# Interleaving two stages of a fused attention and MoE kernel batch by batch, with units of 256 and 320 tokens

## The chip, the cores and the metric

One core of one Trainium2 chip runs the whole program. The metric is device time in microseconds of one execution; a kernel's time is the median of its runs. The engines are TensorE (PE; its weight loads are PEld), VectorE (DVE), ScalarE (ACT), GpSimd (POOL) and SyncE (SP, which issues the DMAs).

## The reference

Three layers follow one another for 4 batches of 576 tokens: causal attention with 8 heads of 64, a gated MoE of width 512 to 1024, and a second MoE that mixes tokens.

```python
scores = np.where(causal, -1000000000.0, scale * q @ k.T + np.minimum(bias, 0.0))
attn = softmax(scores) @ v
x_prev = np.concatenate([zeros, x[:, :-1, :]], axis=1)
xk = mu_k * x + (1.0 - mu_k) * x_prev
xr = mu_r * x + (1.0 - mu_r) * x_prev
k = np.maximum(xk @ w_k, 0.0)
x = 1.0 / (1.0 + np.exp(-(xr @ w_r))) * (k * k @ w_v)
h = np.maximum(x @ w_in, 0.0)
u, v = h[..., :512], h[..., 512:]
v_n = (v - mu) / np.sqrt(var + 1e-06)
v_s = np.einsum('ts,bsd->btd', w_spatial, v_n) + b_spatial[None, :, None]
out = (u * v_s) @ w_out
```

The third layer needs all 576 tokens of one batch (the `einsum` runs over tokens), but nothing of another batch.

## The kernel before

*Precision.* Most products are made of fp16 pairs: an operand is scaled by a power of two and split into a high and a low part (`two_parts`, L652 and L653), and three matmuls give high x high, high x low and low x high. The scales come from the largest absolute value (`power_of_two`, L307 to L320): a reduce on VectorE, a broadcast matmul against the identity, four short VectorE steps.

*Attention* is a list of `steps`: loads and splits of a head, items and products with the values. An item (`do_item`) makes the scores of one head (TensorE), finds the row minimum (VectorE, L454), takes the exponential (ScalarE, L459), divides (L471, L474), writes a high part (L496) and a low part (VectorE, L500) and transposes both by DMA (L502). G0 items hold the first 256 tokens, G1 items tokens 256 to 511, T items the last 64 of two heads. `pv` multiplies with the values (L552, L534) and writes x.

*First MoE.* It runs over nine units of 256 tokens, in the order A0, A1, B0, B1, A2, A3, B2, T, B3: A is the first 256 tokens of a batch, B the next 256, T the last 64 of all four. The first two use fp32 matmuls, the others fp16 pairs. `prep_mix` makes the mixes, then come 20 groups: 8 of `moe_A` (L754), 4 of `moe_B` (the gate, always fp32, L796) and 8 of `moe_C` (L822). A loop over these 180 groups sets the order of the work: after each, `target` says how many attention steps have to be done by then, and jobs that bring in weights are fed in between. Results go to memory (`x2_d`).

*Value sizes.* `value_sizes` loads the values of all batches and reduces them (L341) once, early.

*Second MoE.* When every unit is done, the pools of attention and of the first MoE are closed, and the four batches follow: `moe_Dv` (the half that is normalised, 128 tokens at a time, 512 columns, L1316; its `evac` is the chain L1324 to L1335 on ScalarE and VectorE), `moe_Du` (L1350), `moe_E` (over tokens, L1374), `split_g`, `moe_F` (L1402) and a store. The last 64 tokens of two batches share one tile of `moe_Dv`, so there are 18 tiles. It has all eight PSUM banks, two tiles for the chain (`vrl`) and three for outputs (`o32`).

A scheduler then orders the instructions of each engine; what it made is quoted below where it matters.

## Time and profile before

| | |
|---|---|
| median of 3 runs | 708.95 us (706.0 to 709.26) |
| the profiled execution | 709.66 us, span from first to last instruction 707.9 us |
| mean granted clock of TensorE | 0.954 |
| busy: TensorE, VectorE, ScalarE, GpSimd | 89%, 73%, 58%, 29% of the span |

Busy time is the union of an engine's instructions. Matmuls are pipelined and their ends are modelled, so a busy TensorE may be far from its peak; instruction times on VectorE overlap a little, so their sum is more than its busy time.

### The profile page before, as it was taken

The numbers are of one execution on the slowest core, as the hardware profiler recorded it, in microseconds if no ns is written. First come the engines' busy times: TensorE is split into PE (matmuls) and PEld (weight loads), VectorE is DVE, ScalarE is ACT, GpSimd is POOL, SyncE is SP. The second block draws the span as 40 slices with busy tenths as digits, with TensorE's granted clock in tenths as the row PEclk, the third lists the DMA queues.
The fourth block names the chain that finished last, engine by engine and source line by source line (L and its number), as shares of the span: only waits on it lengthen the run. The fifth ranks groups of instructions, "written<-read, shape, count | busy, mean of one in ns | idle before, by whom it ended". The sixth has DMA issues, their size and how long they took to land. (4 is left out here: it accounts for less than half of the span.)

```text
span 707.9 us, 12975 instructions
## 1 busy us (share of the span) xinstructions
PE 631.2 (89%) x4664; PEld 498.6 (70%) x4664; DVE 516.6 (73%) x1247; ACT 409.1 (58%) x930; POOL 206.6 (29%) x229
## 2 busy tenths in 40 slices
PE   3656979999769989988899889799999999999998
PEld 2444757887658868876688677588767676776786
DVE  7989868978998977999898974934765707527223
ACT  2533797887577578785696682624542723633414
POOL 6120353243451147657357554010200000000000
PEclk9975987999999989999999999899999999999999
DMA  7999966379697666596698675004400100100101
GB/s 188 301 305 343 252 170 142 88 185 203 168 196 177 152 144 128 136 241 149 146 201 195 149 116 137 16 16 149 132 32 1 44 26 1 68 1 1 68 1 68
DMA packets 138953, 92.68 MB, mean 131 GB/s; under 512 B 111268, under 2 KB 121700, under 8 KB 138888
## 3 DMA queue, kind: packets, MB, share of 16 engines
q1 hardware_dynamic: 138888, 91.84, 52.3%
q8 instruction: 37, 0.61, 0.4%
q14 instruction: 28, 0.23, 0.1%
HBM read 55.89 MB, written 9.68 MB: 93 GB/s over the span
## 5 line engine op out<-in xcount | busy, mean ns | idle before, releaser
L459 ACT ACTIVATE sps<-sps,st 128x256 f32<-128x256 f32 (+3 forms) x128 | 64.5, 506 | 56.9 <-DVE st L454 35.5
L754 PE MATMUL mmps<-xp,wkp 128*128 128x256 f16 x672 | 87.5, 287 | 5.5 <-DVE xp L653 2.5
L496 ACT ACTIVATE P<-sps,st 128x128 f16<-128x128 f32 (+3 forms) x128 | 60.6, 531 | 40.5 <-issue 17.5
L754 PEld LDWEIGHTS <-wkp 128*128 128x128 f16 x672 | 66.9, 103 | 21.4 <-issue 9.5
L822 PE MATMUL mmps<-sq,wvp 128*128 128x256 f16 x672 | 80.9, 277 | 0.9 <-DVE sq L787 0.9
L227 POOL TENSOR_TENSOR kl<-raw,kh 64x576 fp32r<-64x576 f32 (+1 forms) x40 | 54.0, 1351 | 71.8 <-ACT kh L263 52.2
L822 PEld LDWEIGHTS <-wvp 128*128 128x128 f16 x672 | 65.0, 99 | 12.9 <-issue 2.0
L500 DVE SCALAR_TENSOR_TENSOR P<-sps,st,P 128x128 f16<-128x128 f32 (+3 forms) x128 | 65.2, 544 | 8.0 <-ACT P L496 7.8
L454 DVE CUSTOM_DVE_ANT_0 sps<-sps,mask 128x128 f32<-128x128 f32 (+3 forms) x128 | 62.1, 497 | 8.7 <-PE sps L435 7.6
L796 PE MATMUL mmps<-xm,wr 128*128 128x256 f32 x288 | 67.4, 386 | 0.0
L796 PEld LDWEIGHTS mmps<-xm,wr 128*128 128x128 f32 x288 | 54.7, 194 | 7.4
L1379 DVE TENSOR_TENSOR g<-dps,uu 128x288 f32<-128x288 f32 x32 | 14.4, 455 | 59.2 <-PE dps L1374 59.2
L430 PE MATMUL sps<-raw 66*128 66x128 f32 (+1 forms) x96 | 28.4, 449 | 26.9 <-DVE P L500 12.5
L1350 PE MATMUL dps<-x,wi 128*128 128x288 f16 x384 | 48.0, 286 | 0.0
L1402 PE MATMUL dps<-gh,wo 128*128 128x288 f16 x256 | 47.9, 286 | 0.0
L1350 PEld LDWEIGHTS <-wi 128*128 128x128 f16 x384 | 37.6, 98 | 10.0
L1402 PEld LDWEIGHTS <-wo 128*128 128x128 f16 x384 | 37.6, 98 | 10.0
L1316 PE MATMUL dps<-wi,x 128*128 128x512 f16 x192 | 42.9, 379 | 0.0
L227 POOL TENSOR_TENSOR qh<-raw,qh 64x320 fp32r<-64x320 f32 (+1 forms) x40 | 41.6, 1041 | 0.2
L430 PEld LDWEIGHTS sps<-raw 66*128 66x128 f32 x96 | 18.3, 258 | 31.6 <-DVE P L500 15.4
L652 ACT ACTIVATE gh<-g,vmg 128x288 f16<-128x288 f32 x32 | 14.5, 526 | 42.6 <-DVE vmg L320 42.6
L434 PE MATMUL sps<-kh,qh 128*128 128x384 f32 (+1 forms) x80 | 34.4, 435 | 3.3 <-POOL qh L227 2.1
(257 smaller groups left out, 1506.6 us busy)
## 6 DMA issues: line engine op xcount, KB each, us to landing
raw<-in_qkb_dram SPq DMA_DIRECT2D x32, 448.0 KB
va<-in_v_dram SPq DMA_DIRECT2D x4, 1280.0 KB
vr<-in_v_dram SPq DMA_DIRECT2D x16, 320.0 KB
raw<-x_d SPq DMA_DIRECT2D x4, 1152.0 KB
out_dram<-o SPq DMA_DIRECT2D x32, 144.0 KB
b<-in_w_v_dram SPq DMA_DIRECT2D x8, 512.0 KB
stage<-in_w_in_dram SPq DMA_DIRECT2D x8, 512.0 KB
x_d<-xo SPq DMA_DIRECT2D x16, 256.0 KB
```

The source lines that it names most:

```text
L227: nc.gpsimd.tensor_tensor(out=out, in0=in0, in1=in1, op=ALU.subtract)
L430: nc.tensor.matmul(o, q[:, 0, g, 128 * t:128 * t + 128], q[:, 1, g, 0:W], start=True, stop=True)
L454: nc.vector.tensor_tensor_reduce(out=self.ps[i], in0=self.ps[i], in1=mask[:, 512 - W:512], scale=-0.125, scalar=3.0e38, op0=ALU.add, op1=A ...
L459: nc.scalar.activation(out=self.ps[i], in_=self.ps[i], func=AF.Exp, scale=-1.0, bias=st[:, i:i + 1], accum_out=st[:, 2 + i:3 + i])
L496: nc.scalar.activation(out=hi, in_=ein, func=AF.Copy, scale=r)
L500: nc.vector.scalar_tensor_tensor(out=lo, in0=ein, scalar=r, in1=hi, op0=ALU.mult, op1=ALU.subtract)
L754: nc.tensor.matmul(out, w, a, start=(i == 0), stop=(i == len(pairs) - 1))
L796: nc.tensor.matmul(columns(ps, m), W["r"][:, k, 128 * m:128 * m + 128], mix[u, "r"][:, k], start=(k == 0), stop=(k == 3))
L822: nc.tensor.matmul(columns(ps, m), weight("v", l, u)[:, k, 128 * m:128 * m + 128], pick(sq[u, k // 2], a, u)[:, k % 2], start=(k == 0 and ...
L1316: nc.tensor.matmul(ps, a[:, k, j:j + 128], w[:, k, 512:1024], start=(n == 0), stop=(n == 11))
L1350: nc.tensor.matmul(ps[:, 0:HB], w[:, k, 128 * m:128 * m + 128], a[:, k, HB * hf:HB * hf + HB], start=(n == 0), stop=(n == 11))
L1402: nc.tensor.matmul(ps[:, 0:HB], w[:, k, 128 * m:128 * m + 128], a[:, k], start=(n == 0), stop=(n == 11))
```

## The change

The first MoE has eight units, A of 256 and B of 320 tokens for each batch; there is no unit T. `MAIN` gives the order of units and of the second MoE of each batch: M0 stands between A1 and B1, M1 between A2 and B2, the first part of M2 (all but F) between A3 and B3, its F and M3 at the end. One loop runs over all groups, with an estimated duration for each, and `marks` and `limits` tie the attention steps to that clock. The weights of the second MoE are brought in from 40 to 120 of these estimated microseconds. Pools aren't closed any more: mixes, gates, results, weights on arrival and most of the second MoE share seven work tiles (`work`), the squares and the normalised half share one `pair_tile`, and the chain of `moe_Dv`, outputs and square remainders share two small tiles. The second MoE gets three PSUM banks (`MMB`). The buffers of P fall from 3 to 2, of `eT2` from 3 to 2, of x from 3 to 2.

`moe_Dv` runs five tiles for each batch, the last of 64 tokens. Sizes are found where the data is: of the values by batch (`size_part`, `size_rest`, `size_all`), of a unit's result by unit. All first halves of the values use five products of bf16 parts, where batches 2 and 3 had three of fp16. Some work changes engine (`X_ACT`, `V_STT`, `V_POOL`, `QUP_POOL`, `SQ_POOL`, `NORM_ACT`).

```diff
+X_ACT = ('10', '11', '12', '13', '20', '22', '23', 'T3')
+V_POOL = (0, 1)
+QUP_POOL = ('1', '2', '3')
+MIX_POOL = ('rB3',)
+SQ_POOL = (0, 3, 4, 5, 7)
+NORM_ACT = ('G1',)
+MAIN = ('A0', 'B0', 'A1', 'M0', 'B1', 'A2', 'M1', 'B2', 'A3', 'M2a', 'B3', 'M2b', 'M3')
+NAT_U = 2
+MKS = (0, 0, 4, 2, 0, 0, 0)
+PREP_K = 5
+PREP_R = 4
+X2_LOAD = 16
+X2_SPLIT = 3
...
-PB = 3
+PAD_POS = 9
+LATER_0 = 40.0
+LATER_1 = 120.0
-T2B = 3
+T2B = 2
 RB = 2
-XB = 3
+XB = 2
+PB = 2
+W5 = 7
+B2B = 2
...
+    def work():
+        return mp.tile([128, 1284], F32, tag="w5", name="w5", bufs=W5)
+
+    def work32(n, c=4):
+        return work()[:, 0:c * n].rearrange("p (c n) -> p c n", c=c)
+
+    def work16(n):
+        return work()[:, 0:4 * n].bitcast(F16).rearrange("p (l c n) -> p l c n", l=2, c=4)
+
+    def pair_tile():
+        return mp.tile([128, 5120], F16, tag="sq", name="sq")
+
+    def small(n):
+        return mp.tile([128, 512], F32, tag="b2", name="b2", bufs=B2B)[:, 0:n]
+
...
+    def size_part(b, i, x):
+        made.add(("vmax", b, i))
+        nc.vector.tensor_reduce(
+            out=vmax[:, b, i:i + 1], in_=x, axis=mybir.AxisListType.XY, op=ALU.max,
+            apply_absolute_value=True)
+
+    def size_rest(b, i):
+        t = work()[:, 0:768].rearrange("p (g n) -> p g n", g=2)
+        nc.sync.dma_start(
+            out=t.rearrange("p g (c n) -> p g c n", c=3),
+            in_=v[b, 2 * i:2 * i + 2, :, 2:5].rearrange("g p c n -> p g c n"))
+        return lambda: size_part(b, 4 + i, t)
+
+    def size_all(b):
+        assert all(("vmax", b, i) in made for i in range(6))
+        vm = vsize[b] = wp.tile([128, 4], F32, name=f"vsize{b}")
+        power_of_two(vm, vmax[:, b], bank(), mybir.AxisListType.X)
+        nc.vector.tensor_scalar(
+            out=vm[:, 1:2], in0=vm[:, 2:3], scalar1=1.0 / PSC, scalar2=None, op0=ALU.mult)
+
     def v_first_load(b, p):
...
+            if key not in xo:
+                xo[key] = work32(n)
+            j = slice(m + 1 - nb, m + 1)
+            nc.vector.tensor_tensor(
+                out=xo[key][:, j].rearrange("p a n -> p (a n)"), in0=whole(ps, key),
+                in1=rg[key][:, j].rearrange("p a n -> p (a n)"), op=ALU.mult)
+            if m == 3:
+                vm = vmx[key] = wp.tile([128, 4], F32, name=f"vmx{key}")
+                power_of_two(vm, xo[key], bank())
+                if key not in DIRECT:
+                    nc.sync.dma_start(out=x2_part(key), in_=xo.pop(key))
...
+    def load_x2(key):
+        if key in DIRECT:
+            return
+        t = xo[key] = work32(width(key))
+        nc.sync.dma_start(out=t, in_=x2_part(key))
+
+    def split_x2(key):
+
+        n = width(key)
+        t = wp.tile([128, 2, 4, n], F16, tag="x2" + key[0], name="x2" + key[0])
+        hi, lo = x2[key] = [t[:, l] for l in range(2)]
+        vm, raw = vmx[key], xo.pop(key)
+        for c in range(0, 4, 2):
+            two_parts(hi[:, c:c + 2], lo[:, c:c + 2], raw[:, c:c + 2], vm[:, 3:4])
+        u = un[key] = wp.tile([128, 2], F32, name=f"un{key}")
+        nc.vector.tensor_scalar(
+            out=u[:, 0:1], in0=vm[:, 2:3], scalar1=P2["w_un"], scalar2=0.5, op0=ALU.mult,
+            op1=ALU.mult)
...
-        ps = pq.tile([128, 512], F32, tag="mm", name="dps", bufs=8)
+        key = half_key(b, i >= 2)
+        j, r = (128 * (i % 2), 128) if i < 4 else (QA, 64)
+        ps = mm_bank()
...
-            for w, a in passes(W["in"], x2[b] if i < 4 else xt2):
-                j = 128 * i if i < 4 else 0
+            for w, a in passes(W["in"], x2[key]):
                 nc.tensor.matmul(
-                    ps, a[:, k, j:j + 128], w[:, k, 512:1024], start=(n == 0), stop=(n == 11))
+                    ps[0:r], a[:, k, j:j + r], w[:, k, 512:1024], start=(n == 0), stop=(n == 11))
...
+            if i == 0:
+                t = pair_tile()[:, 0:8 * DM].rearrange("p (l c n) -> p l c n", l=2, c=4)
+                vn[b] = [t[:, l] for l in range(2)]
+            q = slice(0, r)
+            vr = small(512)[q]
+            st = mp.tile([128, 12], F32, tag="lst", name="lst", bufs=2)[q]
+            nc.scalar.activation(out=vr, in_=ps[q], func=AF.Relu, scale=un[key][q, 0:1])
...
-            for j in range(2):
-                a, o = half(j), half(1 - j)
-                for t in (te[j], tf[j]):
-                    nc.scalar.activation(out=t[a], in_=vr[a], func=AF.Copy)
-                nc.vector.tensor_tensor(out=te[j][o], in0=vr[a], in1=tf[j][a], op=ALU.subtract)
+            for t in (te, tf):
+                nc.scalar.activation(out=t[dn], in_=vr, func=AF.Copy)
+            nc.vector.tensor_tensor(out=te[up], in0=vr, in1=tf[dn], op=ALU.subtract)
...
-            o = pa.tile([128, HB], F32, tag="o32", name="o32", bufs=3)
-            nc.scalar.activation(
-                out=o, in_=ps[:, 0:HB], func=AF.Copy, scale=gt[b, hf][1])
-            nc.sync.dma_start(
-                out=out[128 * m:128 * m + 128, b * S + HB * hf:b * S + HB * hf + HB], in_=o)
+            o = small(nn)
+            nc.scalar.activation(out=o, in_=ps[:, 0:nn], func=AF.Copy, scale=gt[key][1])
+            c = b * S + QA * hf
+            nc.sync.dma_start(out=out[128 * m:128 * m + 128, c:c + nn], in_=o)
...
+    def second_groups(st):
+        b, part = int(st[1]), st[2:]
+        out = []
+        if part != "b":
+            out += [((moe_Dv, b, i), 2592.0) for i in range(5)]
+            for hf in range(2):
+                out += [((moe_Du, b, m, hf), 12 * 0.425 * (QA, QB)[hf]) for m in range(4)]
+            for hf in range(2):
+                out += [((moe_E, b, m, hf), 14 * 0.425 * (QA, QB)[hf]) for m in range(4)]
+        if part != "a":
+            for hf in range(2):
+                out += [((moe_F, b, m, hf), 12 * 0.425 * (QA, QB)[hf]) for m in range(4)]
+        return out
+
+    groups, start_of = [], {}
+    for st in MAIN:
+        start_of[st] = len(groups)
+        groups += second_groups(st) if st[0] == "M" else unit_groups(st)
...
+    marks = [(0.0, pos[0])]
+    limits = []
+    for i, key in enumerate(units[1:]):
+        g = start_of[key]
+        at(g - PREP_K, prep_mix, key, "k")
+        at(g - PREP_R, prep_mix, key, "r")
+        marks.append((max(clock[max(g - PREP_K, 0)] - MKS[i], marks[-1][0] + 0.1), ends[key]))
+        if i + 1 + XB < len(units):
+            limits.append((max(g - PREP_R, 0), first_use[units[i + 1 + XB]]))
+        g = start_of.get(f"M{b}", start_of.get(f"M{b}a"))
+        for key in (f"A{b}", f"B{b}"):
+            at(g - X2_LOAD, load_x2, key)
+            at(g - X2_SPLIT, split_x2, key)
+    for st in MAIN:
+        if st[0] == "M":
+            g, b = start_of[st], int(st[1])
+            if st[2:] != "b":
+                at(g + 18, split_g, b, 0)
+                at(g + 22, split_g, b, 1)
...
+    for gi, ((f, *args), cost) in enumerate(groups):
+        while pend and f not in (moe_Dv, moe_Du, moe_E, moe_F):
+            pend.pop(0)()
+        for g, a in todo.pop(gi, ()):
+            while pend:
+                pend.pop(0)()
+            if g is prep_mix:
+                att_to(ends[a[0]])
+            g(*a)
+        if wjobs or wq:
+            weights(2 if gi < W_FAST else W_RATE)
+        ev = f(*args)
+        while pend:
+            pend.pop(0)()
+        if ev:
+            if f in (moe_A, moe_B, moe_C):
+                ev()
+            else:
+                pend.append(ev)
+        n = target(clock[gi + 1])
+        for g, s_ in limits:
+            if gi < g:
+                n = min(n, s_)
+        att_to(n)
+        if not wjobs and not wq or gone:
+            want = (clock[gi + 1] - LATER_0) / (LATER_1 - LATER_0) * n_later
+            while later and gone < want:
+                if not wjobs:
+                    wjobs.append(later.pop(0))
+                weights(1, 1)
+                gone += 1
```

TensorE, inside the second MoE of batch 0. `x_5641` and `x2A`, `x2B` are the scaled result of the first MoE, `wi` the weights, `sps` a bank of scores, `eT` and `vhl` operands of a product with the values. Before:

```order
L1350 LDWEIGHTS wi
L1350 MATMUL dps<-x_5641,wi 128x288
L1316 LDWEIGHTS xth
L1316 MATMUL dps<-wi,xth 128x512
L1316 LDWEIGHTS xtl
L1316 MATMUL dps<-wi,xtl 128x512
```

Now, with rows of batch 1's attention (a T item, the next product with the values) between two groups of `moe_Du`:

```order
L1208 LDWEIGHTS wi
L1208 MATMUL mmps<-x2A,wi 128x256
L386 MATMUL sps<-kh,qh 128x288
L387 MATMUL sps<-kl,ql 128x288
L386 MATMUL sps<-kh,qh 128x288
L387 MATMUL sps<-kl,ql 128x288
L517 LDWEIGHTS vhl
L517 MATMUL pvps<-eT_2277,vhl 64x256
L1208 LDWEIGHTS wi
L1208 MATMUL mmps<-x2B,wi 128x320
```

Before, nothing but second MoE stood in this part of TensorE's list; now scores and products of the next batch stand in it.

ScalarE, the start of the same chain (`vrl`, now `b`, is the normalised half, `lst` its statistics). Before:

```order
L1324 ACTIVATE vrl<-dps,un_5642 128x512
L1327 ACT_TABLE_LOAD
L1327 ACTIVATE lst<-lst,eps 128x1
L1324 ACTIVATE vrl<-dps,un_5642 128x512
L1334 ACTIVATE vnh<-vrl 128x512
L1324 ACTIVATE vrl<-dps,un_5642 128x512
L1327 ACTIVATE lst<-lst,eps 128x1 x2
L1361 ACTIVATE uu<-dps,un_5642 128x288
```

Now, among a G1 item's parts (L467), a head's split (L258, L259) and an exponential of a T item (L419):

```order
L467 ACTIVATE P<-sps,st 128x512
L1181 ACTIVATE b_2609<-mmps,unA_2434 128x512
L1184 ACT_TABLE_LOAD
L1184 ACTIVATE lst<-lst,eps 128x1 x2
L258 ACTIVATE kh<-raw 128x576
L259 ACTIVATE qh<-raw 128x320
L1192 ACTIVATE sq<-b_2581 128x512
L1192 ACTIVATE sq<-b_2609 128x512
L419 ACT_TABLE_LOAD
L419 ACTIVATE e,st<-e,st 128x576
```

The square root and the exponential each bring a table load when they take turns; the later list has 18 of them, the earlier one 2.

VectorE, at the last product of unit A0 (`xo<-rg,mmps`, now `w<-mmps,w`). Before:

```order
L445 ISA e,st<-sps,maskt,st 128x288
L445 ISA st 128x1
L653 SCALAR_TENSOR_TENSOR wvp<-wv,wsc,wvp 128x512
L833 SCALAR_TENSOR_TENSOR xo<-rg,mmps 128x512
L471 TENSOR_SCALAR st<-st 128x2
L561 TENSOR_SCALAR xt<-pvps,vsize 64x64
L474 RECIPROCAL st<-st 128x2
```

Now:

```order
L471 SCALAR_TENSOR_TENSOR P<-sps,st,P 128x128
L605 SCALAR_TENSOR_TENSOR w_1333<-w_1331,muk,x 128x320 x4
L749 TENSOR_TENSOR w_1344<-mmps,w_1116 128x512
L605 SCALAR_TENSOR_TENSOR w_1350<-w_1331,mur,x 128x320 x4
L471 SCALAR_TENSOR_TENSOR P<-sps,st,P 128x256
L749 TENSOR_TENSOR w_1344<-mmps,w_1116 128x512
L282 TENSOR_REDUCE vmax<-vr 128x1
L471 SCALAR_TENSOR_TENSOR P<-sps,st,P 128x128
L471 SCALAR_TENSOR_TENSOR P<-sps,st,P 128x256
L282 TENSOR_REDUCE vmax<-w_1454 128x1
```

Around it stood a G1 and a T item of batch 0 and the weights' conversion; now it is G0 items of batch 1 (128 and 256 columns), the mixes of B0 and value sizes of batch 1.

## Rows read from the trace of the kernel before

**Rows 1.** The page, busy us, share of the span and instructions by engine.

```profile
span 707.9 us, 12975 instructions
PE 631.2 (89%) x4664; PEld 498.6 (70%) x4664; DVE 516.6 (73%) x1247; ACT 409.1 (58%) x930; POOL 206.6 (29%) x229
```

**Rows 2.** By stage: length; busy us (instructions); granted clock; DMA share; GB/s.

```profile
0.00:135.30 135.30, 96.75 (x519) 74.17 (x520) 116.44 (x319) 79.59 (x204) 41.15 (x66) 0.85 0.83 228
135.30:250.00 114.70, 102.91 (x785) 85.89 (x783) 101.74 (x250) 78.99 (x181) 42.91 (x41) 1.00 0.79 178
250.00:441.00 191.00, 174.19 (x1455) 144.16 (x1455) 161.24 (x383) 135.47 (x326) 112.14 (x113) 0.96 0.72 159
441.00:507.00 66.00, 59.64 (x457) 51.84 (x457) 42.89 (x70) 32.52 (x53) 10.45 (x12) 0.95 0.22 72
507.00:707.90 200.90, 197.75 (x1452) 142.59 (x1450) 94.28 (x229) 82.57 (x169) 0.00 (x0) 1.00 0.09 32
420.00:440.00 20.00, 20.00 (x183) 17.19 (x182) 8.76 (x17) 7.04 (x16) 6.45 (x6) 1.00 0.64 134
```

**Rows 3.** The chain that ended last: start us, us, what.

```profile
478.64 10.48 PE mmps L754 x96
...
489.12 3.46 PE mmps L796 x16
...
506.96 10.36 PE dps L1316 x48
...
568.17 11.76 PE dps L1350 x96
...
704.83 0.50 ACT o L1408
```

**Rows 4.** Timeline of TensorE at the end of unit A0: start us, us, what.

```profile
129.76 5.34 PE L822 MATMUL mmps<-sq,wv 128*128 128x256 f32 x24
```

**Rows 5.** Waits of TensorE: us in total, times, longest.

```profile
PE sps L430 <- DVE P L500: 12.5, 7, 6.1
```

**Rows 6.** VectorE by line and shape: busy us, mean ns | idle before.

```profile
L471 DVE TENSOR_SCALAR st<-st 128x2 f32<-128x2 f32 x64 | 22.6, 355 | 8.7 <-ACT sps L459 8.4
...
L787 DVE TENSOR_TENSOR sq<-mmps,sq 128x512 f16<-128x512 f32 x21 | 14.4, 687 | 10.1 <-ACT mmps L786 10.1
...
L341 DVE TENSOR_REDUCE vsize<-va 128x1 f32<-128x2560 f32 x4 | 11.3, 2817 | 2.8 <-DMA va<-in_v_dram 2.8
...
L379 DVE SCALAR_TENSOR_TENSOR vhl<-vr,vsize,vhl 128x256 f16<-128x256 f32 x8 | 7.1, 892 | 0.1
```

**Rows 7.** The chain of `moe_Dv` on both engines, by line and shape.

```profile
L1325 DVE BATCH_NORM_STATS2 lst<-vrl 128x6 f32<-128x512 f32 x18 | 12.5, 693 | 21.8 <-ACT vrl L1324 21.6
...
L1335 DVE TENSOR_TENSOR vnl<-vrl,vnh 128x512 f16<-128x512 f32 x16 | 10.8, 688 | 3.2 <-ACT vnh L1334 3.1
...
L1330 DVE TENSOR_SCALAR vrl<-vrl,lst 128x512 f32<-128x512 f32 x18 | 9.7, 540 | 0.5
...
L1326 DVE BATCH_NORM_AGGREGATE lst<-lst 128x2 f32<-128x6 f32 x18 | 3.2, 180 | 0.2
...
L1329 DVE RECIPROCAL lst<-lst 128x1 f32<-128x1 f32 x18 | 2.8, 158 | 3.4 <-ACT lst L1327 3.4
...
L1324 ACT ACTIVATE vrl<-dps,un 128x512 f32<-128x512 f32 x16 | 10.9, 681 | 22.6 <-PE dps L1316 16.4 <-DVE lst L1326 6.2
...
L1334 ACT ACTIVATE vnh<-vrl 128x512 f16<-128x512 f32 x16 | 9.8, 625 | 1.2 <-DVE vrl L1330 1.0
...
L1327 ACT ACTIVATE lst<-lst,eps 128x1 f32<-128x1 f32 x18 | 5.3, 293 | 6.9 <-DVE lst L1326 4.0 <-DVE vmx L320 2.0 <-DVE vmg L320 1.0
...
L1327 ACT ACT_TABLE_LOAD x1 | 1.3, 1283 | 0.0
```

More of the change, by code (lines that the diff above doesn't have):

```diff
@@ L625, in load_weights @@
             out.append(job)
-        return full, out
+        return out
     def col_blocks(kc, n, step=128):
@@ L637 @@
     mu = {}
[L638 to L649 removed]
+    for nm in "kr":
+        mu[nm] = wp.tile([128, 4], F32, name="mu" + nm)
     def two_parts(hi, lo, x, by):
@@ L778, in evac @@
[L778 to L783 removed]
+            if key not in sq:
+                t = pair_tile()
+                sq[key] = (
+                    t[:, 0:16 * n].bitcast(F32).rearrange("p (m n) -> p m n", m=8)
+                    if native(key) else t[:, 0:16 * n].rearrange("p (l m n) -> p l m n", l=2, m=8))
@@ new lines, in evac @@
+            o, j = whole(ps, key), slice(m + 1 - nb, m + 1)
+            if native(key):
+                nc.scalar.activation(out=o, in_=o, func=AF.Relu)
+                nc.scalar.activation(
+                    out=sq[key][:, j].rearrange("p a n -> p (a n)"), in_=o, func=AF.Square)
+                return
+            nc.scalar.activation(out=o, in_=o, func=AF.Relu, scale=wsc[:, 10:11])
+            hi, lo = (sq[key][:, l, j].rearrange("p a n -> p (a n)") for l in range(2))
+            nc.scalar.activation(out=hi, in_=o, func=AF.Square)
@@ L941 @@
             add(load_head, b, 2 * p + 1)
+            if p == 0:
+                for i in range(2):
+                    add(rest_size, b, i)
+                add(size_all, b)
             add(prep_v_split, b, p)
@@ L994 @@
             nc.sync.dma_start(out=mu[nm], in_=src.rearrange("(c p) -> p c", p=128))
-        for i in range(W_PRE):
+        for i in range(W_PRE - 2):
             wq.append(wjobs.pop(0)())
     cum_parts()
-    while pos[0] < ends[ORDER[0]]:
+    while pos[0] < ends[units[0]]:
         att_to(pos[0] + 3)
@@ L1276 @@
-    assert prep2 is not None and not later
-    for f in prep2:
-        f[1]()
-    m1.close()
-    ps1.close()
-    pa = ctx.enter_context(tc.tile_pool(name="moe2", bufs=1, side="left", reuse_waits="tile"))
-    pq = ctx.enter_context(tc.tile_pool(name="ps2", bufs=1, space=PSUM, reuse_waits="tile"))
-    spare[0] = lambda: pq.tile([128, 512], F32, tag="mm", name="vps", bufs=8)
-    pw = P2["pool"]
-    wsh, wsl = P2["ws"]
-    ws1, ws2, s_un = P2["ws1"], P2["ws2"], P2["s_un"]
-    vnh, vnl = (pa.tile([128, 4, DM], F16, name="vn" + l) for l in "hl")
@@ new lines, in now, with open_loads, job @@
+        def now(f, *args):
+            return lambda: lambda: f(*args)
+        jobs = []
+        def open_loads(f):
+            def job():
+                loads = f()
+                wjobs[0:0] = loads
+                return None
+            return job
+        jobs.append(open_loads(in_loads))
+        jobs.append(now(size_in))
+        jobs += [now(in_parts, i) for i in range(8)]
+        jobs.append(open_loads(out_loads))
+        jobs.append(now(size_out))
+        jobs += [now(block_parts, i, "out", "o_by") for i in range(4)]
@@ new lines, in later_weights @@
+        jobs += [lambda c=c: sp_size(c) for c in range(5)]
+        jobs.append(now(sp_all))
+        jobs += [lambda c=c: sp_parts(c) for c in range(5)]
+        return jobs
+    te, tf = (wp.tile([128, DM], F16, name=nm) for nm in ("te", "tf"))
+    nc.gpsimd.memset(tf[up], 0.0)
+    for j in range(2):
+        nc.gpsimd.memset(tf[64 + 32 * j:65 + 32 * j], VSC)
+    eps = wp.tile([128, 1], F32, name="eps")
+    nc.vector.memset(eps, 1e-6 / VSC ** 2)
+    x2, un, uu, gt, vn = {}, {}, {}, {}, {}
@@ L1447 @@
+    while pend:
+        pend.pop(0)()
+    assert pos[0] == len(steps) and not later and not wjobs and not wq and not todo
 def kernel(**inputs):
```

781 lines of the change are left out of this document (284 added, 497 removed).

## The prediction

> **What bounds the kernel now.** I read the shares of the engines first. TensorE is busy for 89% of the span, VectorE for 73%, ScalarE for 58% [rows 1]. These are averages over two very different halves, so the table by stage comes next [rows 2]. Up to 441 us (attention and the first MoE) VectorE is busy 116.4 of 135.3, then 101.7 of 114.7, then 161.2 of 191.0 us: 86, 89 and 84%. After 507 us (second MoE) it is busy 94.3 of 200.9 us, 47%, while TensorE hardly pauses. So the first part is held by VectorE, the last by TensorE, and each leaves the other engine's time unused.
>
> A busy TensorE is not one at its peak, so I price its work from stretches in which it runs without a pause [rows 3]: 96 fp16 matmuls of 256 columns take 10.48 us, 96 of 288 take 11.76, 48 of 512 take 10.36; about 0.425 ns a column. Gate matmuls in fp32 (recorded twice each) take 3.46 us for 8: 1.69 ns a column. With the program's counts the work before is:
> - two fp32 units of 256 tokens, 80 matmuls of 0.433 us each: 2 x 34.6 = 69.2;
> - seven fp16 units, 192 x 0.109 + 16 x 0.433 = 27.9 each: 195.3;
> - scores 58, products with the values 71, sums and sizes 8 (their columns at the same prices): 137;
> - second MoE: 216 matmuls of 512 columns, 46.6, and 1,216 of 288, 149.0: 195.6.
>
> Together 597 us. Of the span of 707.9 us 111 us are lost to idling, slow clock and slow starts. Cut at the ends of stages, with the work that the order has in each: up to the end of unit A0 at 135.1 us [rows 4], 72.5 of work, 63 lost; to 250 us, 104 of work, 11 lost; to 441, 166 of work, 25 lost; to 507, 56.5 of work, 9.5 lost; the rest 198 of 201, 3 lost. The losses after 135 us (48 us) are what the change can reach: there TensorE waits for attention and its VectorE work while four batches of second MoE have not been started. The waits agree: TensorE's scores wait for VectorE's last read of a score bank, up to 6.1 us at a time in the head [rows 5].
>
> **The change, part by part.** *TensorE's work.* No tail unit: 320-token units replace 256 + tail with the same columns. The two fp32 units now hold 576 tokens, not 512: 64 tokens x (64 x 1.69 - 192 x 0.425) = 1.7 us more. The normalising product runs five tiles for each batch, not 18 in all: 24 matmuls of 512 columns, 24 x 0.216 = 5.2. Batches 2 and 3 take five instead of three products in the first half of the values: 64 matmuls, half of 256, half of 128 columns, 5.2. Four more size broadcasts of 128 fp32 columns: 0.9. Sum +13.0: work 610.
>
> *VectorE's work* [rows 6]. Four reduces of 2.82 us go; 16 of 256 and 8 of 768 columns and four short chains come, 3 us more. Half of the divisors go to ScalarE (32 x 0.355 = -11.4), eight value splits go (8 x 0.892 = -7.1), most square remainders go to GpSimd (21 x 0.687 to some 6.5: -7.9). Sizes by unit, wider mixes and two more normalising tiles add about 10. Sum -13: 504 us.
>
> *ScalarE* gets the divisors (32 x 0.29 = 9.3) and 16 more table loads (18 in its order, 2 before), 16 x 1.283 = 20.5 [rows 7]; the rest cancels to some 8 less. 409 becomes 431 us, 62%: covered, except inside the normalising chain (second rival). GpSimd goes from 207 to about 240 us, 35%; nothing waits for its sum.
>
> *Up to the end of A0.* VectorE's list ahead of A0's last product weighs the same: instruction times from the trace add to 152 us, to 150 before, although the value sizes are spread out, because more attention now stands ahead of it (13 G0, 8 G1 and 4 T items; before 16, 5 and 3). Those 150 took 116.4 busy and 135.1 us of time, so I keep 63 us lost and put the end of A0 (71 us of work) at 134 us. Bounds: 9 us earlier if the removed reduces (11.3 us) all come off the path, a few later if B0's attention goes first.
>
> *From A0 to the last E of batch 0*, TensorE has 131 us of work (B0, A1, M0). VectorE has A1's and part of B1's attention, the second MoE's weights (now due by then) and M0's evacuations: 153 us of instruction times; the stretch to 250 us had 121 on that scale and was 101.7 busy, so this is 128 busy. At that stretch's density (89%) it takes 144 us; TensorE loses 13. End: 278 us.
>
> *From there on* TensorE has 610 - 71 - 131 = 408 us, VectorE some 250, 60%. Here the gain lies: second MoE fills what attention leaves open, and after the last attention item only about 100 us are left. The loss has no row of its own. The lower end is 1.5% (3 of 201 us, second MoE alone), the upper 13% (25 of 191 us, VectorE at 84%). (The 66 us to 507 lost 14% with VectorE at 65%, but to the second MoE's operands and the tail's mix, which now come earlier or not at all.) I take 2%, 8 us, since VectorE is at 60%; in the 20 us from 420 us, with VectorE at 44%, attention and unit ran side by side with TensorE at 20.0 of 20 [rows 2].
>
> *Moved waits.* Each unit's result goes through memory and is fetched 16 groups ahead of use; the store was issued a whole unit earlier, so the load waits for a work tile, not for data. Behind it on SP's queue stand the loads and transposes of attention, which is why I don't take the lower bound. The second MoE's output tile now comes from two shared tiles: 0.50 us of evacuation and 2.6 to the end of the span for the store [rows 3], so a group each 1.55 us against 1.31 of work in the 256-column half: 16 x 0.24 = 4 us if all of it showed; three banks hide most.
>
> Sum: 134 + 144 + 408 + 8 + 3 (store at the end) = 697 us span. The profiled execution took 709.66 with a span of 707.9, so 1.8 is added: 698.8. That execution lies 0.7 above the median of 708.95, so I say **698**.
>
> **The rivals.**
> *The head shrinks too.* The loads of all the values and 11.3 us of reduces leave the head. If A0 ends 9 us earlier and nothing but the 3 us at the end is lost after batch 0, the span is 680 and the time 681. For it: the reduces stood among the items of the head. Against it: VectorE's list ahead of A0's end is not shorter.
>
> *Slower: the normalising chain starves TensorE.* In batches 0 to 2 each tile of it now shares ScalarE and VectorE with attention, and only two tiles and three banks hold it. Its eight links add to 3.86 us [rows 7], under twice the 2.59 us of its matmuls; it hides as long as it stays under 5.2. If every link also waits behind one attention instruction (about 0.42 us, busy time over count in [rows 1]) and the square root brings two table loads (2.57), it takes 9.8, so 4.9 a tile: 2.3 us lost on each of 15 tiles, 35 us. If attention's matmuls fill half of that, 17 us, and the output tile costs its 4, the time is 719. For it: 17 loads in the later order stand between exponentials and square roots. Against it: the units' matmuls that lie ready in the queue. By the Trainium skill (ScalarE: Activation LUTs, What ACT_TABLE_LOAD costs) a switch of sets costs a drain on top of the load, 2.66 us in all; by that the chain would be an estimated 12.6 us and this rival end at 730, and no row here shows the drain. The Trainium skill (Perfetto Trace Analysis, Matmul Optimizations) asks for all eight banks of PSUM; the change takes the second MoE from eight to three, and with eight this trace lost 3 of 201 us there.
>
> *Nothing comes of it.* The shared work tiles (seven) carry mixes, results, weights on arrival and second MoE. If a batch's second MoE gets its tiles only halfway through the next unit, the filler comes late and TensorE keeps half of the 13% lost before 441 us: 6.5% over the 308 us of work between batch 0 and the last 100 us, 21 us in place of 8. The time is 711, no change. For it: every mix, result and weight block asks for one of the seven. Against it: they are held for less than a unit each.
>
> **How the numbers follow.** About 0.5%, 3.5 us, is what a measurement of this kernel can tell from no change; so faster means under 705.4, slower over 712.5. Forecast 0.48, with 688 to 707 as its own range (the head's bounds, and a loss of 0 to 4% after batch 0): 0.43 of it counts as faster, 0.05 as same. Head shrinks 0.15, all faster. Starved 0.27, slower. Nothing 0.10, same. So faster 0.58, same 0.15, slower 0.27. The range reaches from 681 (first rival) to 720 (second).
>
> **What would show it.** Right: A0's last product near 134 us; M0's last E near 278 with VectorE near 89% busy; then TensorE above 95% busy at full clock with VectorE near 60%; about 100 us of pure TensorE at the end. Wrong: repeated gaps of TensorE in the normalising product that end with ScalarE or with the square root's tile (second rival); idle time that ends with a work tile's load (third); a head that is over by 125 us (first). The forecast as a whole is wrong if TensorE loses more than 16 us after the end of batch 0.

## The result and the profile after

The changed kernel takes 713.76 us (median of 19 runs), the kernel before 707.78 us on the same chip: a ratio of 1.0075, 95% interval 1.0056 to 1.0094. It is slower by 0.75%, where 698 us were forecast; the forecast's own mark for slower was 712.5.

The page's span and busy time by engine answer to [rows 1]:

```profile
span 712.5 us, 12822 instructions
PE 642.0 (90%) x4536; PEld 477.8 (67%) x4536; DVE 503.6 (71%) x1249; ACT 424.7 (60%) x983; POOL 241.8 (34%) x264
```

Over the whole span these three engines were busy as forecast: VectorE 503.6 us (504), ScalarE 424.7 (431), GpSimd 241.8 (240). So the time was lost to waiting. The table by stage (columns as in [rows 2]) is cut at A0's last product (128.6 us) and at M0's last product of `moe_E` (309.0 us); three stretches inside the middle stage follow, the last from `moe_E`'s first product on:

```profile
0.00:128.60 128.60, 91.04 (x505) 70.23 (x505) 114.97 (x283) 78.61 (x188) 59.87 (x73) 0.89 0.71 194
128.60:309.00 180.40, 160.16 (x1019) 115.82 (x1019) 152.58 (x367) 104.88 (x241) 62.30 (x56) 0.92 0.59 152
309.00:712.50 403.50, 390.76 (x3013) 291.72 (x3012) 236.09 (x601) 241.16 (x554) 119.65 (x135) 1.00 0.39 94
...
128.60:143.00 14.40, 9.57 (x72) 7.13 (x72) 9.61 (x44) 9.21 (x32) 2.89 (x2) 0.63 0.67 130
143.00:160.00 17.00, 17.00 (x69) 11.13 (x70) 11.80 (x30) 5.99 (x18) 1.66 (x2) 0.81 0.88 274
...
290.90:309.00 18.10, 16.55 (x138) 13.01 (x136) 12.45 (x38) 9.20 (x23) 0.00 (x0) 1.00 0.43 85
```

After 309 us the forecast holds: TensorE idles 12.7 of 403.5 us (403.50 - 390.76), at full clock. Between A0 and M0's end it does not: TensorE is 20.2 us idle (180.40 - 160.16), and its 160.2 busy us ran at a granted clock of 0.92, worth another 12.8. TensorE's timeline shows where (in brackets the idle time before the row and what ended it):

```profile
126.71 1.89 PE L738 MATMUL mmps<-sq,wv 128*128 128x256 f32 x8
...
142.96 1.44 PE L661 MATMUL mmps<-w,wk 128*128 128x320 f32 x2 [0.87 <-DVE w L605]
...
194.05 0.49 PE L323 MATMUL vps<-ident,vmw 128*128 128x128 f32 x2 [2.09 <-DVE vmw L320]
...
214.84 4.20 PE L661 MATMUL mmps<-w,wkp 128*128 128x256 f16 x24 [2.51 <-ACT b L692]
220.72 7.17 PE L706 MATMUL mmps<-w,wr 128*128 128x256 f32 x32 [1.68 <-DVE sq L696]
...
233.86 1.00 PE L499 MATMUL pvps<-eTt,vhl 128*128 128x128 f16 x15 [4.00 <-DMA eTt<-P]
...
271.59 5.76 PE L1208 MATMUL mmps<-x2A,wi 128*128 128x256 f16 x36 [2.02 <-ACT b L1181]
```

A0 ends at 128.6 us and B0 starts at 142.96. In these 14.4 us TensorE has only scores and products of attention, at a granted clock of 0.63 (a mean between its levels of 1.2 and 2.4 GHz), and in the next 17 it is at 0.81, though always busy. Before, A1 followed A0 without a gap:

```profile
129.76 5.34 PE L822 MATMUL mmps<-sq,wv 128*128 128x256 f32 x24
134.94 1.89 PE L754 MATMUL mmps<-xm,wk 128*128 128x256 f32 x8
```

The later gaps shown are 1.7 to 4.0 us long and end with VectorE, ScalarE or a transpose by DMA. The gaps don't point at one engine.

### The profile page after: what moved, and what is told of

Its sections match the earlier page's. It is cut to its first block, busy times and chain, and to the rows that moved or that the text cites. A ratio compares the mean times of both kernels' runs of the same rounds, so it can differ in the third digit from the quotient of the medians.

```text
span 712.5 us, 12822 instructions
## 1 busy us (share of the span) xinstructions
PE 642.0 (90%) x4536; PEld 477.8 (67%) x4536; DVE 503.6 (71%) x1249; ACT 424.7 (60%) x983; POOL 241.8 (34%) x264
## 5 line engine op out<-in xcount | busy, mean ns | idle before, releaser
L430 ACT ACTIVATE sps<-sps,st 128x128 f32<-128x128 f32 (+3 forms) x128 | 64.4, 504 | 55.6 <-DVE st L425 36.8
L467 ACT ACTIVATE P<-sps,st 128x128 f16<-128x128 f32 (+3 forms) x128 | 60.9, 530 | 43.7 <-DMA eT<-P 19.2
L661 PE MATMUL mmps<-w,wkp 128*128 128x320 f16 (+1 forms) x576 | 77.3, 291 | 2.9 <-ACT b L692 2.5
L738 PE MATMUL mmps<-sq,wvp 128*128 128x320 f16 (+1 forms) x576 | 75.8, 290 | 0.0
L425 DVE CUSTOM_DVE_ANT_0 sps<-sps,mask 128x128 f32<-128x128 f32 (+3 forms) x128 | 61.7, 499 | 14.4 <-PE sps L406 7.3
L706 PE MATMUL mmps<-w,wr 128*128 128x256 f32 (+1 forms) x256 | 66.2, 410 | 1.7 <-DVE sq L696 1.7
L706 PEld LDWEIGHTS mmps<-w,wr 128*128 128x128 f32 x256 | 47.4, 190 | 14.5 <-DVE sq L696 2.0
L661 PE MATMUL mmps<-w,wk 128*128 128x256 f32 (+1 forms) x128 | 42.2, 487 | 15.4 <-DVE w L629 9.2
L661 PE MATMUL mmps<-wo,sq 128*128 128x256 f16 (+1 forms) x256 | 49.4, 289 | 5.5 <-DVE w L1239 4.0
L1264 PE MATMUL mmps<-w,wo 128*128 128x320 f16 (+1 forms) x384 | 50.4, 286 | 1.0 <-ACT w L576 0.5
L661 PEld LDWEIGHTS <-sq 128*128 128x128 f16 x384 | 37.4, 99 | 15.5 <-issue 5.9
L661 PEld LDWEIGHTS mmps<-w,wk 128*128 128x128 f32 x128 | 27.9, 227 | 25.8 <-DVE w L629 10.6
L1264 PEld LDWEIGHTS <-wo 128*128 128x128 f16 x384 | 36.9, 98 | 11.6 <-issue 2.0
L661 PE MATMUL mmps<-wsl,sq 128*128 128x256 f16 (+1 forms) x128 | 37.1, 290 | 0.0
```

Of the source, the lines that this page charges most:

```text
L425: nc.vector.tensor_tensor_reduce(out=self.ps[i], in0=self.ps[i], in1=mask[:, 512 - W:512], scale=-0.125, scalar=3.0e38, op0=ALU.add, op1=A ...
L430: nc.scalar.activation(out=self.ps[i], in_=self.ps[i], func=AF.Exp, scale=-1.0, bias=st[:, i:i + 1], accum_out=st[:, 2 + i:3 + i])
L467: nc.scalar.activation(out=hi, in_=ein, func=AF.Copy, scale=r)
L661: nc.tensor.matmul(out, w, a, start=(i == 0), stop=(i == len(pairs) - 1))
L706: nc.tensor.matmul(columns(ps, key, m), W["r"][:, k, 128 * m:128 * m + 128], mix[key, "r"][:, k], start=(k == 0), stop=(k == 3))
L738: nc.tensor.matmul(columns(ps, key, m), weight("v", l, key)[:, k, 128 * m:128 * m + 128], pick(sq[key], a, key)[:, k], start=(k == 0 and q ...
```

## The experiments

All ratios are to the kernel before, run on the same chip beside each kernel. A warning first: a scheduler orders all engines' instructions anew for each kernel, so an edit's price holds what the new order does. In one run below (no table switch) the traces show TensorE's and VectorE's instructions in the same order throughout; in the decode cut about 7% of TensorE's matmuls and 10% of VectorE's instructions stand elsewhere, in others more.

### What the interleaving is worth

```diff
-MAIN = ('A0', 'B0', 'A1', 'M0', 'B1', 'A2', 'M1', 'B2', 'A3', 'M2a', 'B3', 'M2b', 'M3')
+MAIN = ('A0', 'B0', 'A1', 'B1', 'A2', 'B2', 'A3', 'B3', 'M0', 'M1', 'M2', 'M3')
...
-LATER_0 = 40.0
-LATER_1 = 120.0
+LATER_0 = 60.0
+LATER_1 = 300.0
```

> Undoes the interleaving alone: A0 B0 A1 B1 A2 B2 A3 B3 and then the four second MoEs, with everything else of the change left in (320-token units, value sizes by batch, shared work tiles, three banks); weights from 60 to 300 of the estimated microseconds. Theory F: the weights leave the front, which gains about 30 us, and the filler is lost, which costs what attention then leaves open (before the change 25 + 9.5 us from 250 to 507 us): 700 to 720. If the 320-token units and the smaller buffers are themselves the cost (U, B): 720 to 740.

Measured: 772.73 us, 1.0894 (1.0857 to 1.0932). So interleaving, with the later weights that go with undoing it, is worth some 57 us, more than the 40 of the forecast (48 lost after A0, 8 kept), and everything else in the change costs 63. By stage, that kernel ends its units at 556 us (before 507) and needs 215 us for the second MoE (before 200.9, [rows 2]). Three stretches show what the units lost:

```profile
250.00:282.00 32.00, 19.11 (x153) 14.61 (x154) 22.62 (x78) 17.73 (x51) 6.94 (x8) 0.75 0.71 139
...
389.00:404.00 15.00, 5.94 (x70) 4.80 (x70) 10.14 (x24) 7.83 (x22) 7.90 (x10) 0.72 0.63 156
499.00:516.00 17.00, 2.85 (x39) 2.48 (x40) 8.38 (x8) 2.29 (x4) 8.20 (x4) 0.67 0.18 36
```

These are holes ahead of B1, B2 and B3. In the first two the A unit is done and the B unit's attention (eight G1 and four T items) is not. In the third the attention is nearly done, and most of the hole is a wait for the unit's mixes, which end with ScalarE's split (L576):

```profile
516.22 0.96 PE L661 MATMUL mmps<-w,wkp 128*128 128x320 f16 x3 [10.81 <-ACT w L576]
```

TensorE is busy 27.9 of 64 us in the three, and VectorE is not full either (41 of 64). M0, M1 and M2a stand exactly there in the changed kernel. So, by this reading, the interleaving mostly fills holes that the new arrangement opens. Both expectations fall: even units and buffers (U, B) were put at 740 at most.

Two runs put M0 later, the second M1 too:

```diff
+MAIN = ('A0', 'B0', 'A1', 'B1', 'M0', 'A2', 'M1', 'B2', 'A3', 'M2a', 'B3', 'M2b', 'M3')
+LATER_0 = 60.0
+LATER_1 = 165.0
```

> The second MoE of batch 0 comes one unit later (after B1, not after A1), and its weights are brought in from 60 to 165 of the estimated microseconds, not from 40 to 120. Theory F (front load): between 129 us (A0's last product) and 309 us (M0's last product of moe_E) TensorE has some 135 us of work and takes 180, because VectorE has to turn the second MoE's weights into fp16 pairs there (about 58 us of its instruction time) on top of attention. With the weights spread over more units the time falls by 12 to 30 us: 683 to 702. Theory U (the unit): the loss is that of B0 as a 320-token unit in fp32, whose order and precision stay: 708 to 718. Theory B (buffers): P, eT2 and x have lost a buffer each, attention cannot run ahead: 708 to 718.

```diff
+MAIN = ('A0', 'B0', 'A1', 'B1', 'A2', 'M0', 'B2', 'M1', 'A3', 'M2a', 'B3', 'M2b', 'M3')
+LATER_0 = 100.0
+LATER_1 = 195.0
```

> The second MoE of batch 0 comes after A2, that of batch 1 after B2, and the weights are brought in from 100 to 195 of the estimated microseconds. Theory F: VectorE has only attention and units until some 200 us and the weights fall where TensorE has A2 and M0; the time falls by 15 to 35 us, to 678 to 698, and A1 and B1 end earlier than 250 and 376 us. Theory U and theory B: the first 300 us keep their losses, less filler work in between: 708 to 722.

Measured: 744.54 us, 1.0497 (1.0456 to 1.0537), and 754.15, 1.0631 (1.0595 to 1.0667). Both lie above every range that they were given. Theory F (front load) forecast a gain, and none came; but these runs move M0 as well as the weights, and the hole ahead of B1 is open again. In the first of the two the stretch ahead of B1 reads

```profile
243.00:292.00 49.00, 26.95 (x169) 19.79 (x167) 38.48 (x101) 23.63 (x60) 16.86 (x16) 0.56 0.52 107
```

TensorE is busy 26.95 of 49 us, at a granted clock of 0.56. The next run tests theory F without moving M0.

### Is VectorE's load the bound ahead of M0?

```diff
+        if not all_steps:
+            return
         nc.vector.scalar_tensor_tensor(
             out=d, in0=hi_w, scalar=-0x40000000, in1=d, op0=ALU.bitwise_and, op1=ALU.bitwise_or)
...
+                return lambda: (made.add((name, i)), load_double(full[:, ks, ns], raw, name not in ("win", "wo")))
```

> Leaves out two of the three VectorE steps that decode w_in and w_out (12 blocks; in the trace after 16 + 8 instructions of 0.67 to 1.16 us, 23.8 us in all); signs and low bits of these weights are lost, every transfer and wait stays. Theory F: VectorE sets the pace there at 85% busy, so M0's last moe_E product comes 18 to 28 us earlier than 309 us and the time falls to 688 to 697. Theories U and B: VectorE's work on weights lies beside TensorE's, and less than 6 us are won: 707 to 715.

Measured: 714.91 us, 1.0072 (1.0041 to 1.0103), as the changed kernel. M0's last product of `moe_E` came at 310 us, with 309 in the changed kernel, although VectorE had 136.0 us to do since 128.6, not 152.6:

```profile
128.60:200.00 71.40, 66.58 (x330) 45.47 (x329) 49.92 (x146) 34.14 (x97) 27.33 (x25) 0.90 0.65 176
200.00:248.00 48.00, 40.78 (x321) 34.10 (x320) 41.09 (x91) 31.92 (x67) 19.89 (x20) 0.93 0.88 218
248.00:310.00 62.00, 52.61 (x378) 36.19 (x376) 45.03 (x116) 44.20 (x85) 12.34 (x12) 0.94 0.38 74
```

VectorE falls from 85% to 75% busy and the stage is as long. Its amount of work is not the bound there, and theory F falls.

### The cut buffers

```diff
-PB = 3
+PB = 2
...
-T2B = 3
+T2B = 2
...
-XB = 3
+XB = 2
```

in the kernel before, and nothing else:

> The kernel before with the buffers of P, of eT2 and of x cut from 3 to 2, as the change cuts them, and nothing else. With the second MoEs last the rest of the change costs 63 us against before (772.7 against 709.5). Theory B (buffers): these three cuts are most of it, since attention's items then wait for one another: 730 to 770. Theory U (units): the pairing of short A and long B units is it, and the buffers cost little: 707 to 716.

Measured: 732.34 us, 1.0355 (1.0312 to 1.0398): 25 us, at the low end of what theory B expected. Cut at the same marks as the first three of [rows 2] (the ends of A0, B0 and B2) its table reads

```profile
0.00:141.60 141.60, 95.87 (x518) 74.34 (x519) 116.93 (x316) 77.18 (x199) 42.62 (x65) 0.82 0.81 218
141.60:248.10 106.50, 97.88 (x717) 82.23 (x716) 90.48 (x214) 74.31 (x163) 40.69 (x37) 0.98 0.74 172
248.10:458.00 209.90, 186.19 (x1525) 151.46 (x1525) 169.00 (x420) 142.02 (x347) 111.77 (x115) 0.93 0.67 151
```

The same VectorE work (516.5 us in all, before 516.6) is stretched: the stage from B0's end to B2's takes 209.9 us where it took 191, at 80% of VectorE in place of 84; the stage ahead of it is 8 us shorter, A0's 6 longer. Where the wait sits is in the view of waits: ScalarE, which writes P's high part, waits for a transpose that still reads the buffer (us in total, times, longest). In order, the kernel before, the same with the cut buffers, the changed kernel, and the changed kernel with three buffers of P (the next run):

```profile
ACT P L496 <- DMA eT<-P: 5.6, 1, 5.6
...
ACT P L496 <- DMA eT<-P: 24.1, 15, 5.8
ACT P L496 <- DMA eTt<-P: 17.9, 10, 3.3
...
ACT P L467 <- DMA eT<-P: 19.2, 9, 5.6
ACT P L467 <- DMA eTt<-P: 12.5, 3, 9.0
...
ACT P L467 <- DMA eT<-P: 0.6, 1, 0.6
```

So the wait is 5.6 us with three buffers and 42.0 with two, and the changed kernel has 31.7 us of it. Putting buffers back into the changed kernel, at the price of a work tile, was tried twice, once with P alone and once (B0 in fp16) with P and eT2:

```diff
-PB = 2
-W5 = 7
+PB = 3
+W5 = 6
```

> The changed kernel with three buffers of P again, paid for by six work tiles in place of seven. Theory B: attention runs ahead again and 8 to 25 us come back, 689 to 706, unless the work tile costs as much. Theory U: 708 to 720.

> B0 in fp16 pairs, three buffers each of P and of eT2 as before the change, paid for with one of seven work tiles. The cuts cost the kernel before 25 us (P, eT2 and x together). Theory B: 5 to 20 us come back, 688 to 703. If the work tiles bind as hard: 706 to 722.

Measured: 719.30 us, 1.0170 (1.0128 to 1.0211), and 721.98, 1.0212 (1.0175 to 1.0249). Both are slower than with seven work tiles and the cut buffers, although the wait for P is gone. A work tile is worth at least as much as the buffers it would pay for, so what the cuts cost inside the changed kernel is not shown in time; the 25 us hold for the kernel before.

### B0 in fp32, and the order of the first units

```diff
-NAT_U = 2
+NAT_U = 1
```

> The changed kernel with B0 in fp16 pairs and only A0 in fp32. By columns B0 then has 8.7 us less of TensorE's work, VectorE 5 us more, and the buffers of the fp32 weights come free earlier, so the second MoE's weights can start before 168 us. Theory U: TensorE was busy 66 of 74 us in B0 and this comes off the time: 698 to 707. Theory B, or attention beside the unit being the pace: A1's mixes come no earlier and it is 709 to 718.

Measured: 708.39 us, 0.9998 (0.9972 to 1.0025): the change's loss is gone, no more. Of some 8.5 us less work, by the prediction's prices, about 5 show. A part is waited away at the end of B0:

```profile
208.05 1.01 PE L499 MATMUL pvps<-eTt,vhl 128*128 128x128 f16 x15 [1.46 <-DMA eTt<-P]
212.09 0.80 PE L323 MATMUL vps<-ident,vmxB 128*128 128x128 f32 x2 [3.03 <-DVE P L471]
```

> Order A0 A1 B0 B1 M0 A2 M1 B2 A3 M2a B3 M2b M3, weights from 60 to 165 of the estimated microseconds: the fp32 units have 256 tokens again, as before, and the light attention of A1 lies beside A0. Theory S (what lies beside B's attention sets the loss: one unit of 28 us cannot cover B's eight G1 and four T items, one unit and a second MoE can): B0's and B1's attention lie beside A1 and B0 without a second MoE, gaps of 15 to 40 us open ahead of B0 and B1, 728 to 750. Theory U: the 8.7 us of fp32 work and the late start of B0 go, 695 to 707.

Measured: 727.48 us, 1.0276 (1.0235 to 1.0316), just below theory S's range and far from theory U's. It differs from the run with M0 one unit later only in that A1 stands ahead of B0 (and so in 64 fewer fp32 tokens). Each against the kernel before beside it, they lose 35 and 20 us: 15 us for the order of two units.

### Table switches, banks

```diff
-                out=st[:, 8:9], in_=st[:, 7:8], func=AF.Sqrt, bias=eps[q], scale=VSC ** -2)
+                out=st[:, 8:9], in_=st[:, 7:8], func=AF.Relu, bias=eps[q])
```

> The changed kernel (B0 in fp32) with the square root of the normalising chain replaced by a relu of the same shape, so that 18 table loads become 1; the normalised half has other values. Removes 17 x 1.283 = 21.8 us of ScalarE's time, some before exponentials, some in the chain. Theory A: 4 to 12 us of the time, 702 to 710 (713.8 with them). If the loads lie beside other work: 711 to 715.

Measured: 707.77 us, 0.9992 (0.9967 to 1.0016), 6 us less than the changed kernel. The table loads in the changed kernel, by line:

```profile
L1184 ACT ACT_TABLE_LOAD x9 | 11.5, 1283 | 0.2
L430 ACT ACT_TABLE_LOAD x6 | 7.7, 1283 | 0.9 <-PEq L1419 0.8
L419 ACT ACT_TABLE_LOAD x3 | 3.8, 1283 | 0.1
```

17 of these 18 go, 21.8 us of ScalarE, and 6 us of the time, inside theory A's range: the cleanest price here, since the other engines' order is the same. It is the second rival's mechanism, at less than a third of its 21 us. In this trace a switch costs its load and no more, as ScalarE's timeline shows (start, us):

```profile
412.10 0.69 ACT L1181 ACTIVATE b<-mmps,unA 128x512 f32<-128x512 f32 x1 [0.89 <-PE mmps L1170]
412.80 1.28 ACT L1184 ACT_TABLE_LOAD   x1
414.10 0.29 ACT L1184 ACTIVATE lst<-lst,eps 128x1 f32<-128x1 f32 x1
```

The Trainium skill (ScalarE: Activation LUTs, What ACT_TABLE_LOAD costs) has 2.66 us for a switch with its drain; here it is 1.30 (412.80 to 414.10), and the measurement decides.

```diff
-        ps = pq.tile([128, 512], F32, tag="mm", name="dps", bufs=8)
+        ps = pq.tile([128, 512], F32, tag="mm", name="dps", bufs=3)
...
```

> The kernel before with three PSUM banks for the products of the second MoE in place of eight (and four of their own for the size broadcasts), nothing else. With the second MoEs last the changed kernel's second MoE took 221 us (from 550 to 771), before 201 (from 507 to 708); 24 more matmuls of moe_Dv are 5 of the 20. Theory K (banks): TensorE waits for the normalising chain with three banks, and 8 to 18 us more are lost: 716 to 727. Otherwise: 707 to 711.

Measured: 710.47 us, 1.0050 (1.0027 to 1.0074): 3 to 4 us, below what theory K (banks) expected. The Trainium skill's advice to use all eight banks (Perfetto Trace Analysis, Matmul Optimizations) is worth 0.5% here. Of the 14 us by which the second MoE is longer with all of them last (215 us by the trace; the 221 above count from 550 us, inside B3), 5 are work by the prediction's prices, and 3 may be banks, measured on the kernel before; the rest is not settled.

### Moving work between engines and in time

> The changed kernel with the conversion of w_k and w_v to fp16 pairs (16 VectorE steps of 0.7 to 0.8 us, the sums, the bounds) started at the 18th of A0's 20 groups and so beside B0, which still uses fp32. VectorE has 14 of 20 us busy in B0 (140 to 180 us) and was full from 40 to 120. Theory V (VectorE's queue in the head holds B0's attention): B0's first product comes 5 to 12 us earlier than 143 us and the time falls to 700 to 709. If the weights only move from one full stretch into the next (w_in then follows later, still ahead of M0): 709 to 722.

> B0 in fp16 pairs, and the second MoE's weights from 60 to 130 of the estimated microseconds in place of 40 to 120. In the run with B0 in fp16 TensorE idled from 206 to 213 us, while A1's mixes stood in VectorE's queue behind eight splits of w_in (193 to 202 us). Theory Q (order in VectorE's queue): A1 starts 4 to 10 us earlier and the time is 699 to 706 (708.4 with 40 to 120). If M0 then waits for its weights instead: 706 to 718.

> B0 in fp16 pairs, and attention of A1 to be done 8 us and that of B1 10 us (of the estimated clock) ahead of their units, in place of 0 and 4. Theory P (pace by the program's order): A1 starts earlier than 213 us and VectorE is freer from 213 to 251; 702 to 707. If the items only displace the second MoE's weights: 708 to 716.

> B0 in fp16 pairs, and the high part of the T items' P on ScalarE (16 VectorE instructions of 0.66 us off, 16 ScalarE instructions of some 0.8 us on). Theory V (VectorE's amount sets the pace): 10.6 us less of it, 3 to 8 us of the time, 700 to 706. If latency sets it (the decode cut took 24 us off VectorE for nothing): 706 to 712.

> B0 in fp16 pairs, and the divisors of G1 items on VectorE again (32 VectorE instructions of 0.36 us on, 32 ScalarE instructions of 0.29 us off). Theory A (ScalarE's queue sets attention's pace; putting T's high parts there cost 9 us): 2 to 8 us come back, 700 to 706. If VectorE's amount sets it: 710 to 716. If neither: 706 to 710.

Measured, in this order: 725.19 us (1.0238), 721.51 (1.0180), 731.88 (1.0349), 717.25 (1.0126), 713.61 (1.0098); no interval reaches below 1.0069. Every one is slower than the kernel that it edits (713.76 for the first, 708.39 for the other four), and the first four lie above every range that they were given. Moving T's high parts from VectorE to ScalarE loses 9 us, moving the divisors from ScalarE to VectorE loses 5, which is the range given for VectorE's amount setting the pace. Each takes work off one engine and puts about as much on the other, so they show only that a shift gains nothing either way, not which queue sets the pace. The gains that theories V, Q, A and P gave here did not come.

The last two try to beat both kernels: B0 in fp16 and no table switch.

```diff
-            nc.scalar.activation(
-                out=st[:, 8:9], in_=st[:, 7:8], func=AF.Sqrt, bias=eps[q], scale=VSC ** -2)
-            nc.vector.reciprocal(out=st[:, 9:10], in_=st[:, 8:9])
...
+            for _ in range(3):
+                nc.vector.scalar_tensor_tensor(
+                    out=t, in0=y, scalar=half_v, in1=y, op0=ALU.mult, op1=ALU.mult)
+                nc.vector.scalar_tensor_tensor(
+                    out=y, in0=t, scalar=1.5, in1=y, op0=ALU.subtract, op1=ALU.mult)
```

> B0 in fp16 pairs, and the inverse square root of the normalising chain on VectorE (an integer seed and three Newton steps: nine instructions of one column in place of the reciprocal, some 1.2 us for each of 20 tiles) in place of ScalarE's square root, so no table switch is left. If the 5.4 us of the fp16 unit and the 6.0 us of the table switches are separate losses they add up, and VectorE's 24 us lie where TensorE is the bound: 699 to 705, under before. If both came out of the same wait, or the longer chain on VectorE costs what the switches did: 706 to 712.

> The same with three small tiles (chain, outputs, square remainders) in place of two, which just fit. If these two tiles hold the chain (TensorE waits for ScalarE's write of one, 2.7 and 2.5 us in all, in the trace of the change): 2 to 5 us less than with two, 696 to 702. If not: within 1.5 us of the run with two.

Measured: 713.39 us, 1.0060 (1.0037 to 1.0083), and with three small tiles 710.40, 1.0019 (0.9995 to 1.0043). The first is above both ranges given to it: the two gains don't add up when the square root goes to VectorE. The third small tile gives 3 us, the gain expected of it, though the time stays above its 696 to 702. No version here is faster than the kernel before.

## Why the prediction was wrong

**The step that failed** is "From A0 to the last E of batch 0": VectorE's 153 us of instruction times, 128 busy, "at that stretch's density (89%)", were to take 144 us, TensorE was to lose 13, and M0's last E was to come at 278 us. It came at 309.0; the stage took 180.4, 36 us more. In the sum, 14 of these 36 us are a matter of booking: `moe_E`'s own products (4 x 14 x 576 columns, 13.7 us) end at that mark, and the step's 131 us of work had them after it (the 160.16 busy us at 0.92 are 147 of full speed). The other 22 are the error. TensorE lost 33 us there (20.2 idle, 12.8 by the clock), not 13.

In the step's own terms both factors were off. VectorE was busy 152.6 us there, not 128 (12.45 of it beside `moe_E`), and its density was 85%, not 89. With both put right the step would give the measured length, but for the wrong reason: VectorE's amount does not set it. The decode cut showed that: 16.5 us less on VectorE, density 75%, same length. Nor can a density be carried over from one arrangement to another: the kernel before, with buffers cut as the change cuts them, ran its long stage at 80% in place of 84% and lost 25 us, and ScalarE's wait for P's buffers went from 5.6 to 42.0 us. The prediction has no term for these cuts, though the text ahead of it names them.

What I read from the trace, without a run that removes it, is that the largest single loss of the stage is the hole ahead of B0 and the slow clock behind it: 4.8 us idle, then 9.6 busy at 0.63 and 17.0 at 0.81, together 11.6 us of full speed. It looks like the hole of B1, B2 and B3 once more, and it is the only one that has no second MoE to fill it. A third buffer of P alone does not close it: in that run B0 still starts 12 us after A0's end (128.0 to 140.3 us).

**Up to the end of A0**: 134 forecast, 128.6 measured, inside the bounds given (9 earlier to a few later). The first rival had this half right.

**After M0**: 408 + 8 + 3 = 419 forecast, less the 14 of booking 405; 403.5 measured, and 12.7 us idle against the 16 named as the limit. This is the part for which the change was made, and TensorE is kept busy as forecast. The closeness is luck in part: by the work terms below an estimated 14 us of the 408 were not work (79,104 columns at 0.425 in place of 0.25 ns), so the loss was about that much larger than the 11 allowed. The limit of 16 us, the prediction's sign that the forecast as a whole is wrong, watched this stage, and the time was lost in the one ahead of it.

**Sum**: -5 + 22 - 1.5 gives the 15.5 us between 697 and 712.5 of span.

**The work terms** for VectorE, ScalarE and GpSimd held within 2% over the span (VectorE's three stages, 116 + 128 + some 250, left 10 of its 504 out). TensorE's had an error in both kernels: products with the values were priced at 0.425 ns a column. The timeline has

```profile
429.73 1.47 PE L1208 MATMUL mmps<-x2A,wi 128*128 128x256 f16 x12 [0.67 <-ACT b L1181]
431.13 1.34 PE L517 MATMUL pvps<-eT,vhl 128*64 128x256 f16 x24
```

24 of them (18 of 256 and 6 of 128 columns, 5,376) in 1.34 us, 0.25 ns a column. These have 64 output rows (`128*64`); that they overlap is my reading of the rate. If all such products can run at it, an estimated 26 us of the 610 (147,456 columns), and 24 of the 597 (135,168), were never work but loss, and the loss to be explained was larger than the 111 us given. It all but cancels in the difference of the two kernels.

**The rivals.** "Nothing comes of it" was the nearest in time (711). It named the work tiles, and the runs with six of them suggest that they bind, but the filler did not come late: M0's first product (250.16 us) follows A1's last without a gap. The starved chain (719) was right that the change is slower, but not for its reason: the switches cost 6 us, and after M0 TensorE's idle time stayed at 12.7 us. No rival held what happened: the change pays 63 us in its arrangement and gets some 57 back. How the 63 divide is only partly shown: 25 buffers and 3 banks, each measured on the kernel before; the 15 us for the order of two units and the 5 of the fp32 unit were measured on variants of the changed kernel and need not add to them; the extra work is 13 by my sums. The rest stays open.

## What to carry to other kernels

Before pricing a fusion of two stages, price alone what is given up to make room for it (buffers, order of the units, banks): run, or at least sum, the rearranged kernel with the stages still apart. A busy share read from a kernel with three buffers need not hold with two (84% became 80% here). Where no engine is full and the gaps end with several causes, test whether an engine's amount sets the length before scaling by it: here 16.5 us off VectorE bought nothing, and a buffer less in three places cost 25. Put the filler beside the units whose operands come late: with M0 one unit later the time was some 30 us longer.
